# A fused attention and gated MLP kernel: v loaded as fp32 by SyncE and cast on chip, and every engine's order laid out anew

## The chip, the core and the metric

The kernel runs on one core of a Trainium2 chip. Its engines are TensorE (PE in the profile, with PEld for its weight loads), VectorE (DVE), ScalarE (ACT), GpSimd (POOL) and SyncE (SP, which here only issues transfers). The metric is the device time of one execution in microseconds (us), as the median of several runs.

## What is computed

The inputs are q, k and v of shape 8 x 12 x 448 x 64 (batch, heads, positions, width), two vectors of 64 weights, and the weights of a gated MLP. All are fp32.

```python
q_n, k_n = (rmsnorm(q, g_q), rmsnorm(k, g_k))          # x / sqrt(mean(x*x) + 1e-06) * g
scores = scale * np.matmul(q_n, k_n.transpose(0, 1, 3, 2))
attn = np.exp(scores - max); attn = attn / (sum + 1e-09)
x = np.matmul(attn, v)                                  # heads side by side: 8 x 448 x 768
h = np.maximum(x @ w_in, 0.0)
u, v = h[..., :512], h[..., 512:]
v_n = (v - mean) / np.sqrt(var + 1e-06)                 # over the 512
v_s = np.einsum('ts,bsd->btd', w_spatial, v_n) + b_spatial[None, :, None]
return ((u * v_s) @ w_out).astype(np.float32)
```

## The kernel before

The order of the work is written out by hand in one long string, PLAN (lines 20 to 152). Each word calls one function op_X, which issues the instructions of one step, and the tiles, their slots and PSUM banks stand in the word. An engine executes its instructions in the order of the words; between engines only data, reused slots and one helper, `port`, make anything wait. A word is `name.arguments/slots/engine`, with the engines a (ACT), v (DVE), g (POOL) and s (SP). So `N.13.1/0/g` normalizes input 1 (k) of group 13 into slot 0 on POOL.

Heads are worked on in 24 groups of 4 heads, three groups for each batch element. Group 0 is brought in by halves (small letters l, q, r, i, j, n, p, k). The steps of a group G:

- L (op_L, line 293): SP loads q (input 0) or k (input 1) of the group as fp32, 128 partitions x 896, into one of 9 slots `raw`. v comes by op_v (line 314): POOL requests it with a cast to bf16 on the way, straight into the tile `vt`, in one transfer for an even group and in two halves for an odd one.
- Q squares the tile (ACT, DVE or POOL), R sums over each 64 (DVE), I and J take a logarithm and an exponential on ACT, which give 1/rms. N (line 426) multiplies the tile by it and writes bf16 (`nrm`).
- T (line 481): SP issues a transposing transfer of `nrm` from SBUF to SBUF, into `qT` for q and into `kr` for k. Z (line 464 on DVE, 462 on ACT) multiplies `kr` by the weights of g_q and g_k and the scale into `kT`. Groups 0 to 3 are transposed by matmuls instead (P, p) and copied out by K, k.
- S (line 506): 8 matmuls of 64 x 32 give the scores of one unit, 128 x 896 in two PSUM banks. E (line 514): one ACT exponential of 128 x 896 writes bf16. There are 7 units in a group, so 168 of each.
- s, a and b (line 539): matmuls that sum the exponentials and multiply them by v, four to a pass. D and d (lines 558, 562) take 1/sum on ACT as exp(-ln), X (line 568) multiplies on DVE into `xt`.

The MLP of a batch element follows when its three groups are done: V and U (lines 584, 645) are matmuls with the two halves of w_in, c and u their ReLU evictions on ACT or DVE (575, 577), B and A the statistics and the normalization (620, 621, 636, DVE), M and m small ACT steps, H the matmuls with w_spatial (659), G the gating on DVE (664), O the matmuls with w_out (673), o their evictions (361, 363) and t the output transfers (690, SP). The last 64 of the 448 positions go through W (line 608), which works the V tail of one batch element beside the O tail of the one before it on two column halves of TensorE; the O tail lies in partitions 64 to 127.

z words (line 260) are dummy matmuls on an identity. setup (lines 245 to 254) fills constants and makes the identity on POOL. gA, gB, gC build the column of weights `g2_col` from two rows, which ACT's queue requests ahead of everything (241, 242). ws, wi, wo are POOL's casting loads of the weights, Y and y the transposes of w_spatial and their copies.

DVE and POOL steps that read and write SBUF call `port` (around line 284), which makes such a step wait for the last such step of the other engine in the order:

```python
def port(eng, inst):
    other = on_port.get("g" if eng is dve else "v")
    if other is not None:
        sync_dep(inst, other)
    on_port["v" if eng is dve else "g"] = inst
```

The steps that call it are Q, q, N, n on either engine, and A and Z on DVE.

Of the kernel before, what the change touches and what calls it, by code (L numbers as in the profile page):

```python
# [20 lines left out]
setup//v l.1.0/0 ws//g l.0.0/1 v.0.2//g L.1.0/2 v.0.1//g L.1.1/3 z.30/7 l.0.1 l.1.1 L.2.0/4 L.2.1/5 q.1.0/0/v L.4.1/6  # L21
gA//v gB/7 q.0.0/1/v L.3.1/7 z.33/6 r.0.0//v gC//v r.1.0//v Q.1.0/2/a L.4.0/8 i.0//a R.1.0//v j.0//a n.1.0//g
Q.1.1/2/a n.0.0//g p.1.0/7 z.7/6 q.0.1//a R.1.1//v q.1.1//g p.0.0/6 k.1.0/0/a Y.1/5 k.0.0/0/v I.1//a Y.3/7 J.1//a
r.1.1//v y.1//a Y.2/4 N.1.0/0/g Q.2.0/2/a r.0.1//v Y.0/5 y.3//v i.1//a y.2//v Q.2.1/0/a S.0.1/01 R.2.0//v N.1.1/1/g
S.0.0/23 L.3.0/2 j.1//a P.1.0/7 E.0.1/0/a R.2.1//v z.12/6 K.1.0/1/a n.1.1//g P.1.1/1 L.5.0/3 z.7/6 E.0.0/1/a K.1.1/1/v
n.0.1//g p.1.1/0 L.6.1/0 I.2//a S.1.6/67 k.1.1//v S.1.3/12 J.2//a S.1.1/34 L.5.1/1 E.1.6/2/a N.2.0/2/g z.3/f y.0//v
p.0.1/0 E.1.3/3/a S.1.0/67 k.0.1//v z.10/5 E.1.0/4/a v.0.0//g P.2.0/2 N.2.1/3/v L.6.0/4 z.4/5 E.1.1/5/a wi.1.1//g
s.1.0.0/7 S.1.2/01 Q.3.1/1/v wi.0.2//g P.2.1/6 E.1.2/6/a S.1.4/34 wi.1.0//g z.5/5 K.2.0/2/v E.1.4/7/a Q.4.0/2/g
S.0.3/01 K.2.1/2/v s.1.1.0 s.1.2.0 E.0.3/8/a s.1.3.0 R.3.1//v S.1.5/23 a.1.0.0/6 S.0.6/45 E.1.5/9/a a.1.1.0 Q.4.1/0/g
S.0.5/01 R.4.0//v a.1.2.0 E.0.6/a/a s.1.4.0 s.1.5.0 s.1.6.0 S.2.0/23 E.0.5/b/a b.1.0.0/5 wi.0.0//g Q.3.0/1/v b.1.1.0  # L30
b.1.2.0 b.1.3.0 v.0.3//g E.2.0/c/a S.2.2/01 a.0.0.0/4 a.1.3.0 R.3.0//v Q.5.0/2/g a.1.4.0 D.1/0/a a.1.5.0 a.0.1.0
E.2.2/d/a a.1.6.0 S.0.4/23 R.4.1//v z.4/7 I.3//a S.0.2/01 wi.0.1//g J.3//a E.0.4/e/a b.1.4.0 N.3.0/0/v b.1.5.0
wi.1.2//g b.1.6.0 s.0.0.0/7 E.0.2/f/a s.0.1.0 wi.0.3//g s.0.2.0 N.3.1/1/v S.2.4/23 s.0.3.0 wi.1.3//g z.2/b d.1//a
s.0.4.0 S.2.1/01 I.4//a s.0.5.0 X.1.1//v s.0.6.0 J.4//a z.5/b E.2.1/g/a N.4.1/2/g X.1.0//v P.3.0/5 D.0/1/a P.3.1/6
K.3.0/3/v E.2.4/h/a S.2.3/01 s.2.0.0/7 K.3.1/3/v s.2.1.0 N.4.0/3/g T.4.1/0 b.0.0.0/5 E.2.3/i/a b.0.1.0 R.5.0//v
b.0.2.0 s.2.2.0 b.0.3.0 d.0//a S.3.1/23 b.0.4.0 b.0.5.0 E.3.1/j/a Q.5.1/1/g S.2.5/01 T.4.0/1 b.2.0.0/6 b.2.1.0 b.0.6.0
E.2.5/k/a S.2.6/23 X.0.1//v a.0.2.0 z.2/b L.7.1/5 a.0.3.0 E.2.6/4/a b.2.2.0 Q.6.1/0/g R.5.1//v S.3.3/01 s.2.3.0
s.2.4.0 E.3.3/5/a s.2.5.0 S.3.0/23 a.2.0.0/5 a.2.1.0 I.5//a a.2.2.0 a.2.3.0 R.6.1//v J.5//a s.2.6.0 E.3.0/6/a
N.5.1/0/g a.0.4.0 a.2.4.0 a.0.5.0 a.0.6.0 Q.6.0/2/a b.2.3.0 a.2.5.0 X.0.0//v b.2.4.0 b.2.5.0 D.2/0/a b.2.6.0 R.6.0//v
N.5.0/1/g a.2.6.0 T.5.1/1 S.3.2/01 d.2//a S.3.4/23 U.0.2.0/7 E.3.2/3/a X.2.1//v U.0.2.1 V.0.1.0/4 X.2.0//v v.1.1//g  # L40
E.3.4/7/a T.5.0/0 V.0.1.1 Z.4/1/v V.0.1.2 I.6//a U.0.2.2 J.6//a c.0.1//v wb N.6.0/2/g S.4.5/01 S.4.0/56 L.7.0/2
u.0.2//v E.4.5/9/a W.0/4 L.8.1/7 E.4.0/2/a v.1.3//g T.6.0/2 S.4.4/23 c.0.3//v S.4.1/01 v.1.2//g S.4.2/56 E.4.4/1/a
U.0.0.0/7 B.0.1//v L.9.1/6 v.1.0//g U.0.0.1 E.4.1/8/a U.0.0.2 Z.5/0/v V.0.2.0/3 E.4.2/0/a N.6.1/3/g u.0.0//v V.0.2.1
S.5.1/01 S.3.5/45 wx//v S.5.6/67 E.5.1/e/a V.0.2.2 Q.7.1/1/g T.6.1/0 U.0.3.0/2 E.3.5/c/a c.0.2//v U.0.3.1 U.0.3.2
E.5.6/g/a L.8.0/8 S.5.5/01 u.0.3//v Q.7.0/0/g S.5.0/34 s.3.0.0/5 L.10.0/1 E.5.5/d/a s.3.1.0 B.0.3//v S.3.6/67 s.3.2.0
s.3.3.0 E.5.0/b/a s.3.4.0 R.7.1//v S.5.4/01 Q.8.1/2/g V.0.0.0/2 E.3.6/f/a V.0.0.1 R.7.0//v V.0.0.2 E.5.4/a/a s.3.5.0
s.3.6.0 c.0.0//v S.5.2/34 I.7//a b.3.0.0/7 b.3.1.0 J.7//a D.3/1/a b.3.2.0 B.0.0//v N.7.0/0/g a.3.0.0/2 s.4.0.1/10
d.3//a S.5.3/56 a.3.1.0 R.8.1//v s.4.1.1 E.5.3/i/a a.3.2.0 a.3.3.0 a.3.4.0 a.3.5.0 N.7.1/1/g B.0.2//v E.5.2/h/a
T.7.0/3 a.3.6.0 S.4.3/56 b.3.3.0 b.3.4.0 X.3.0//v b.3.5.0 M.0//a b.3.6.0 E.4.3/k/a S.4.6/34 X.3.1//v U.0.1.0/2
v.1.4//g T.7.1/1 m.0//a U.0.1.1 E.4.6/4/a Z.6/2/v wo//g s.4.2.1 s.4.3.1 A.0.2//v s.4.4.1 s.4.5.1 L.9.0/3 A.0.0//v  # L50
s.4.6.1 v.2.0//g A.0.3//v S.6.1/56 L.10.1/4 S.6.4/34 A.0.1//v U.0.1.2 v.2.2//g E.6.4/6/a H.0.0/7 v.3.1//g u.0.1//a
H.0.3/4 D.5/0/a G.0.0//v Q.8.0/1/g E.6.1/j/a H.0.1/2 G.0.3//v D.4/1/a S.6.0/56 G.0.1//v S.6.3/34 a.4.0.1/70 d.4//a
a.4.1.1 R.8.0//v a.4.2.1 E.6.0/3/a b.4.0.1/21 b.4.1.1 b.4.2.1 b.4.3.1 Z.7/3/v E.6.3/5/a b.4.4.1 b.4.5.1 b.4.6.1
Q.10.0/2/g a.4.3.1 d.5//a a.4.4.1 X.4.1//v S.7.3/56 S.7.0/34 I.8//a a.4.5.1 X.5.1//v E.7.3/7/a a.4.6.1 H.0.2/2
X.5.0//v Q.9.1/1/g Q.9.0/0/a X.4.0//v S.7.5/56 S.6.2/01 J.8//a G.0.2//v V.1.1.0/7 E.6.2/c/a R.10.0//v V.1.1.1
N.8.1/2/g V.1.2.0/2 E.7.5/f/a V.1.2.1 R.9.1//v E.7.0/2/a V.1.1.2 N.8.0/3/g V.1.2.2 T.8.1/0 R.9.0//v c.1.1//a S.7.4/01
# [97 lines left out]
"""  # L154


SLOTS = dict(raw=9, sqt=3, nrm=4, qT=4, kr=2, kT=4, et=21, rc=2, vs=2, vn=2, us=2, os=5)


@with_exitstack  # L160
# [572 lines left out]
```

## Time and profile before

| | |
|---|---|
| time, median of 3 runs | 285.55 us (282.64 to 287.17) |
| span of the profiled execution, first to last instruction | 277.8 us, 7.75 us under the median |
| first exponential starts | 18.56 us |
| last exponential starts | 232.5 us |
| granted TensorE clock, mean | 0.997 |
| transfers | 51.14 MB, mean 184 GB/s |

The profile is one execution. Its page gives the busy time of each engine and its share of the span, the span in 40 slices with the busy share in tenths, the groups of like instructions (busy time, mean duration of one in ns, then the idle time just ahead of them and what ended most of it), and the transfers by tile with the median time from issue to landing. The trace behind it answers further questions: who waited for whom, the chain of work that ended last, one tile's instructions, and stretches of time. Durations of overlapping instructions add up to more than the busy time of their engine. A busy TensorE is not at its peak, since matmuls are pipelined: 8 score matmuls that follow one another take 0.19 us, and 0.38 us alone.

### The profile page before, as it was taken

How to read it: one execution, taken by the hardware profiler on the slowest of the kernel's cores; microseconds unless marked ns; L12 is line 12 of the kernel's file. 1: busy time of each engine (PE TensorE's matmuls, PEld its weight loads, DVE VectorE, ACT ScalarE, POOL GpSimd, SP SyncE). 2: the span in 40 equal slices, each digit the busy share in tenths (PEclk: the TensorE clock that was granted, in tenths of full speed). 3: DMA queues.
4: the chain of work that ended last, by engine and by line, in shares of the span. 5: the costliest groups of instructions: out<-in, count | busy, mean ns of one | idle time of the engine just before them, and what ended most of it. 6: DMA issues, size and time to landing. Idle time of an engine off the chain costs nothing. (4 is left out here: it accounts for less than half of the span.)

```text
span 277.8 us, 10117 instructions
## 1 busy us (share of the span) xinstructions
PE 261.4 (94%) x4373; PEld 137.4 (49%) x4373; DVE 198.7 (72%) x351; ACT 216.8 (78%) x353; POOL 155.6 (56%) x130
## 2 busy tenths in 40 slices
PE   4799999979999999999999989999998999999993
PEld 4686464435545455354445444453553545455551
DVE  2478978695997997987995677966975174747740
ACT  1399999878999999998999979998898766420632
POOL 3287987987687598957875758645980000000000
PEclk9999999999999999999999999999999999999998
DMA  6989996999989999899999999966589400014586
GB/s 165 331 264 273 176 174 112 217 163 267 257 144 293 311 245 202 179 253 150 257 212 273 228 257 259 181 93 70 75 136 179 161 2 2 18 41 113 138 272 218
DMA packets 62967, 51.14 MB, mean 184 GB/s; under 512 B 39561, under 2 KB 58506, under 8 KB 62922
## 3 DMA queue, kind: packets, MB, share of 16 engines
q1 hardware_dynamic: 54690, 42.22, 64.5%
q0 software_dynamic: 8224, 8.27, 21.2%
q8 instruction: 34, 0.56, 0.8%
q14 instruction: 11, 0.09, 0.1%
q10 hardware_dynamic: 8, 0.00, 0.0%
HBM read 38.55 MB, written 11.01 MB: 178 GB/s over the span
## 5 line engine op out<-in xcount | busy, mean ns | idle before, releaser
L514 ACT ACTIVATE et<-ps 128x896 bf16<-128x896 f32 x168 | 145.7, 921 | 15.0 <-PE ps L506 13.4
L426 POOL TENSOR_TENSOR nrm<-raw,rs 128x896 bf16<-128x896 f32 x43 | 72.2, 1690 | 25.9 <-ACT rs L411 10.1
L506 PE MATMUL ps<-qT,kT 64*32 64x448 bf16 x1344 | 60.2, 354 | 2.5 <-DMA qT<-nrm 1.9
L382 POOL TENSOR_TENSOR sqt<-raw 128x896 f32<-128x896 f32 (+1 forms) x31 | 50.9, 1654 | 17.2 <-DVE vn L636 7.4
L393 DVE TENSOR_REDUCE ss<-sqt 128x14 f32<-128x896 f32 x46 | 48.4, 1075 | 5.0 <-ACT sqt L380 3.8
L539 PE MATMUL ps<-et,vt 64*32 64x448 bf16 x1344 | 48.4, 350 | 2.8 <-DMA vt<-in_v_dram 2.6
L645 PE MATMUL ps<-xt,w_in 128*128 128x448 bf16 x192 | 43.1, 353 | 0.0
L568 DVE TENSOR_TENSOR xt<-ps,rc 128x448 bf16<-128x448 f32 x48 | 28.3, 620 | 14.9 <-ACT rc L562 8.0
L673 PE MATMUL ps<-w_out,gt 128*128 128x384 bf16 x192 | 36.5, 326 | 0.1
L506 PEld LDWEIGHTS <-kT 64*32 64x32 bf16 x1344 | 21.5, 90 | 29.6 <-issue 22.0
L584 PE MATMUL ps<-w_in,xt 128*128 128x512 bf16 x144 | 35.6, 380 | 0.0
L539 PEld LDWEIGHTS <-vt 64*32 64x32 bf16 x1344 | 23.6, 92 | 17.3 <-DMA vt<-in_v_dram 3.9
L664 DVE TENSOR_TENSOR gt<-ps,us 128x448 bf16<-128x448 f32 x32 | 19.3, 620 | 13.0 <-PE ps L659 8.7
L361 ACT ACTIVATE os<-ps 128x384 f32<-128x384 f32 (+1 forms) x33 | 15.9, 493 | 15.4 <-PE ps L673 14.6
L659 PE MATMUL ps<-w_spT,vn 128*128 128x448 bf16 (+1 forms) x128 | 27.7, 353 | 0.0
L645 PEld LDWEIGHTS <-w_in 128*128 128x128 bf16 x192 | 17.0, 98 | 20.5 <-issue 7.3
L539 PE MATMUL ps<-et,ones 64*32 64x448 bf16 x672 | 26.2, 350 | 0.2 <-ACT et L514 0.2
L673 PEld LDWEIGHTS <-gt 128*128 128x128 bf16 x192 | 18.2, 98 | 15.4 <-issue 2.5
L314 POOL DMA_DIRECT2D vt<-in_v_dram x36 | 24.1, 673 | 0.0
L577 DVE TENSOR_SCALAR vs<-ps 128x512 bf16<-128x512 f32 (+1 forms) x24 | 16.3, 684 | 10.4 <-PE ps L584 6.8
L363 DVE COPY os<-ps 128x384 f32<-128x384 f32 (+1 forms) x31 | 16.9, 554 | 8.9 <-PE ps L673 7.7
L620 DVE BATCH_NORM_STATS2 s<-vs 128x6 f32<-128x512 bf16 (+1 forms) x32 | 21.9, 683 | 1.4 <-ACT vs L575 0.9
(62 smaller groups left out, 253.1 us busy)
## 6 DMA issues: line engine op xcount, KB each, us to landing
out_dram<-os SPq DMA_DIRECT2D x56, 192.0 KB, 3.2
raw<-in_q_dram SPq DMA_DIRECT2D x23, 448.0 KB, 5.5
raw<-in_k_dram SPq DMA_DIRECT2D x23, 448.0 KB, 7.0
vt<-in_v_dram POOLq DMA_DIRECT2D x24, 112.0 KB, 5.2
vt<-in_v_dram POOLq DMA_DIRECT2D x12, 224.0 KB, 7.0
w_in<-in_moe_w_in_dram POOLq DMA_DIRECT2D x8, 192.0 KB, 6.1
w_out<-in_moe_w_out_dram POOLq DMA_DIRECT2D x1, 768.0 KB, 11.3
raw<-in_k_dram SPq DMA_DIRECT2D x2, 224.0 KB, 2.6
```

Of the source, the lines that this page charges most:

```text
L314: pool.dma_start(out=vts[b % 2][64 * halves[0]:64 * halves[0] + 64 * len(halves), g].rearrange("p r c d -> p r (c d)"), in_=src)
L382: port(eng, eng.tensor_tensor(out=t, in0=x, in1=x, op=ALU.mult))
L393: dve.tensor_reduce(out=sss[G % 3][:, i].rearrange("p r c -> p (r c)"), in_=sqt[where.pop(("sq", G, i))].rearrange("p r (c d) -> p (r c) d ...
L426: port(eng, eng.tensor_tensor(out=nrm[sl[0]].rearrange("p c r d -> p r c d"), in0=raw[where["raw", G, i]].rearrange("p r (c d) -> p r c d" ...
L506: pe.matmul(out=ps[at:at + 32, sl[n], 0:S], lhsT=kT[64 * r:64 * r + 64, c, 64 * hh + 32 * x:64 * hh + 32 * x + 32], rhs=qT[64 * r:64 * r + ...
L514: act.activation(out=ets[sl[0]], in_=ps[:, a:b + 1:b - a, 0:S], func=AF.Exp, bias=0.0, scale=1.0)
L539: pe.matmul(out=ps[32 * l:32 * l + 32, where[kind, G][0], 0:S], lhsT=w, rhs=et_of(G, r, c)[at:at + 64], start=(n == 1), stop=(n == C), til ...
L568: dve.tensor_tensor(out=xts[b % 2][:, 2 * g + half, :], in0=ps[:, where.pop(("ab"[half], G))[0], 0:S], in1=rcs[where["rc", G]], op=ALU.mult)
L584: pe.matmul(out=ps[:, bank, :], lhsT=xts[b % 2][:, j, 128 * m:128 * m + 128], rhs=w_in[:, j % 2, j // 2, DH:], start=(n == 1 and j == 2 * ...
L645: pe.matmul(out=ps[:, bank, 0:S], lhsT=w_in[:, j % 2, j // 2, 128 * f:128 * f + 128], rhs=xts[b % 2][:, j, :], start=(n == 1 and j == 2 * ...
L659: pe.matmul(out=ps[:, sl[0], 0:S], lhsT=vns[b % SLOTS["vn"]][rows, m, 128 * f:128 * f + 128], rhs=w_spT[rows, m, :], start=(m == 0), stop= ...
L673: pe.matmul(out=ps[:, sl[0], 0:384], lhsT=gts[b % 2][:, f, 128 * m:128 * m + 128], rhs=w_out[:, f, 384 * h:384 * h + 384], start=(f == 0), ...
```

## The change

v is loaded as fp32 by SP into the slots of `raw`, as input 2 of op_L, and cast on chip into `vt` by a new step F. The two rows of g are requested by POOL behind the identity. w_sp no longer has a tile of its own but lies in the two tiles `gt` of the gating, and `raw` has 10 slots and `et` (the exponentials) 22. The O tail of the last batch element is worked in two column tiles, the first half of its columns in partitions 0 to 63 and the second in 64 to 127, and written out by two transfers. The list of words is new throughout. Counts of words that differ, by engine:

| step | before | after |
|---|---|---|
| L (loads of 448 KB) | 46 | 70, of which 24 are v (12 of them in two transfers) |
| v (POOL's casting loads) | 36 transfers | none |
| F (cast of v) | none | POOL 14, DVE 7, ACT 3 |
| N | POOL 43, DVE 3 | POOL 35, DVE 11 |
| n | POOL 4 | POOL 3, DVE 1 |
| Q | ACT 14, POOL 30, DVE 2 | ACT 9, POOL 32, DVE 5 |
| q | ACT 1, POOL 1, DVE 2 | ACT 3, DVE 1 |
| Z | ACT 2, DVE 18 | ACT 5, DVE 15 |
| K, y | ACT 1 each, DVE 5 and 3 | DVE 6 and 4 |
| c | ACT 8, DVE 24 | ACT 13, DVE 19 |
| u | ACT 9, DVE 23 | ACT 12, DVE 20 |
| o | ACT 33, DVE 31 | ACT 34, DVE 30 |
| dummy matmuls | 124 in 13 words, the last near exponential 20 | 63 in 2 words, at the start |

The new start of the list, and one stretch of the old and of the new list from the N of k of group 22 to its Z:

```
setup//v z.33/0 l.0.0/0 q.0.0/0/v r.0.0//v gl.1//g l.1.0/1 gl.0//g q.1.0/1/a gA//v r.1.0//v l.0.1 q.0.1//a r.0.1//v
i.0//a z.30/1 j.0//a gB/2 n.0.0//v p.0.0/3 L.1.0/2 Q.1.0/2/a L.1.1/3 R.1.0//v n.1.0//g Q.1.1/0/a k.0.0/0/a gC//v
p.1.0/4 R.1.1//v I.1//a J.1//a k.1.0/0/v S.0.1/56 S.0.2/07 ws//g N.1.1/0/v N.1.0/1/g S.0.0/13 P.1.1/2 Y.2/4 L.2.1/4
```

```
old: N.22.1/3/g s.18.0.1/75 s.18.1.1 E.21.2/a/a s.18.2.1 s.18.3.1 s.18.4.1 G.4.1//v s.18.5.1 s.18.6.1 S.21.1/01 c.5.1//v
v.6.1//g T.22.1/0 W.5/632 E.21.1/h/a B.5.1//v N.22.0/0/g D.18/1/a I.23//a O.3.2.1/1 D.19/0/a c.5.3//v J.23//a
...
S.21.5/67 u.5.0//v t.0.0 S.21.6/23 S.20.2/45 E.21.5/5/a Z.22/2/v

new: N.22.1/2/g a.18.5.1 a.18.0.1 S.21.4/06 S.21.3/12 b.18.4.1/75 a.18.4.1 I.23//a J.23//a N.23.0/3/g b.18.1.1 b.18.0.1
E.21.3/3/a X.18.0//v X.19.0//v b.18.3.1 b.18.6.1 b.18.2.1 E.21.4/e/a b.18.5.1 X.18.1//v S.21.6/12 E.21.6/f/a S.21.0/34
S.20.2/06 U.5.0.0/7 U.5.0.1 U.5.3.1/1 X.19.1//v E.20.2/2/a U.5.0.2 T.22.1/1 Z.22/1/v
```

The rest of the diff, cut to its core:

```diff
-SLOTS = dict(raw=9, sqt=3, nrm=4, qT=4, kr=2, kT=4, et=21, rc=2, vs=2, vn=2, us=2, os=5)
+SLOTS = dict(raw=10, sqt=3, nrm=4, qT=4, kr=2, kT=4, et=22, rc=2, vs=2, vn=2, us=2, os=5)
-    w_sp = const.tile([64, C, S], BF, name="w_sp")
+    w_sp = gt_all.rearrange("p n f s -> p (n f) s")[0:64, 0:C]
-        x = (q, k)[i]
+        x = (q, k, v)[i]
-    act.dma_start(out=g_row[:, 0], in_=bass.AP(tensor=g_q.tensor, offset=g_q.offset, ap=[[0, 1], [0, 2], [1, D]]))
-    act.dma_start(out=g_row[:, 1], in_=bass.AP(tensor=g_k.tensor, offset=g_k.offset, ap=[[0, 1], [0, 2], [1, D]]))
...
     def op_L(sl, e, G, i):
         b, g = divmod(G, NG)
         where["raw", G, i] = sl[0]
-        engines[e or "s"].dma_start(out=raw[sl[0]], in_=qk_rows(i, b, g))
+        rows = qk_rows(i, b, g)
+        if i < 2 or not flip(G):
+            engines[e or "s"].dma_start(out=raw[sl[0]], in_=rows)
+            return
+        for half in range(2):
+            src = bass.AP(tensor=rows.tensor, offset=rows.offset + (1 - half) * S * D,
+                          ap=[[C * D, 64], [2 * S * D, 2], [1, C * D]])
+            engines[e or "s"].dma_start(out=raw[sl[0]][64 * half:64 * half + 64], in_=src)
+
+    def op_gl(sl, e, i):
+        x = (g_q, g_k)[i]
+        engines[e].dma_start(out=g_row[:, i], in_=bass.AP(tensor=x.tensor, offset=x.offset, ap=[[0, 1], [0, 2], [1, D]]))
...
-    def op_v(sl, e, b, n):
-        g, halves = v_parts(b)[n]
...
-        pool.dma_start(out=vts[b % 2][64 * halves[0]:64 * halves[0] + 64 * len(halves), g].rearrange("p r c d -> p r (c d)"),
-                       in_=src)
+    def op_F(sl, e, G):
+        b, g = divmod(G, NG)
+        eng = engines[e]
+        dst = vts[b % 2][:, g].rearrange("p r c d -> p r (c d)")
+        src = raw[where["raw", G, 2]]
+        if eng is act:
+            copy(eng, dst, src)
+        else:
+            port(eng, eng.tensor_copy(out=dst, in_=src))
+        where["v", b, g] = {0, 1}
...
+    def tail_at(b, h):
+
+        return 0 if b == B - 1 and h == 0 else 64
...
                 h, f = divmod(n, 4)
-                todo.append(((n + 0.5) / 8, dict(
-                    out=ps[64:128, sl[h - 2], 0:384], lhsT=gts[(b - 1) % 2][:, f, TAIL:],
+                at = tail_at(b - 1, h)
+                todo.append(((f + 0.5 * h if b == B else n + 0.5) / 8, dict(
+                    out=ps[at:at + 64, sl[h - 2], 0:384], lhsT=gts[(b - 1) % 2][:, f, TAIL:],
...
-                    tile_position=(0, 64))))
+                    tile_position=(0, at))))
```

## The prediction

> **What bounds the kernel now.** I read the busy shares first, then the slices, then the waits, the windows, the tile views of the transposed q and k, and last the chain that ended last.
>
> ```profile
> span 277.8 us, 10117 instructions
> ...
> PE 261.4 (94%) x4373; PEld 137.4 (49%) x4373; DVE 198.7 (72%) x351; ACT 216.8 (78%) x353; POOL 155.6 (56%) x130
> ...
> ACT  1399999878999999998999979998898766420632
> POOL 3287987987687598957875758645980000000000
> ...
> DMA  6989996999989999899999999966589400014586
> ```
>
> TensorE shows 94%, but ScalarE (ACT) is at 9 tenths nearly everywhere from slice 2 to slice 33 and falls off only when the attention is over. So there are two stages: attention, in which ACT paces (168 exponentials of 0.92 us), and a last stage of matmuls alone. The DMA engines are nearly full for the first 170 us.
>
> ```profile
> L514 ACT ACTIVATE et<-ps 128x896 bf16<-128x896 f32 x168 | 145.7, 921 | 15.0 <-PE ps L506 13.4
> L426 POOL TENSOR_TENSOR nrm<-raw,rs 128x896 bf16<-128x896 f32 x43 | 72.2, 1690 | 25.9 <-ACT rs L411 10.1
> ...
> L382 POOL TENSOR_TENSOR sqt<-raw 128x896 f32<-128x896 f32 (+1 forms) x31 | 50.9, 1654 | 17.2 <-DVE vn L636 7.4
> ...
> L314 POOL DMA_DIRECT2D vt<-in_v_dram x36 | 24.1, 673 | 0.0
> ```
>
> The last number of a row is idle time ahead of it: ACT waited 13.4 us for scores. GpSimd (POOL) spends 24.1 us only on issuing the 36 loads of v.
>
> ```profile
> kr<-nrm SPq DMA_TRANSPOSE x20, 5.3
> qT<-nrm SPq DMA_TRANSPOSE x20, 4.8
> ```
>
> ```profile
> DMA to landing us min/median/max: 3.3/5.3/9.9
> ```
>
> The second fence is the tile view of kr, the transposed k: from issue to landing 3.3 us at best, 5.3 as a rule. This is the row on which the forecast rests.
>
> ```profile
> 202.32 3.35 POOL nrm L426 x2
> ...
> 207.85 7.97 DMA qT<-nrm
> ...
> 215.95 0.38 PE ps L506 x8
> ```
>
> That is the chain that ended last: POOL normalizes the last q, the transpose lands, scores start, and from there TensorE runs without a gap to the end. Behind the last exponential (232.5 us) there are only matmuls, evictions and 4 us of output transfer.
>
> **The change part by part.** The sum is made against the profiled execution: span 277.8 us. The median of the runs is 285.55, so 7.75 us lie around the span; I keep them.
>
> *Start, -5.5 us.* The first exponential starts at 18.56 now. Its scores were ready to start when the copy of q ended at 15.31, but 49 transposes of w_sp (3.42 us, from 14.58) stand ahead of them, and ACT could not take its first logarithm before it had squared a load that landed at 10.60. The new order sets both aside. It pays with the g rows: POOL requests them after the identity (1.63 us), and the VectorE (DVE) product that needs them stands ahead of the second sum r.1.0. Landed on the queue before they took until 8.18; from POOL I take the same to be safe (bounds: 4 us, the 2.6 us of the fastest small load after an issue at 1.7, and 8.2). Then 0.28 (product) + 0.61 (sum) + 0.29 + 0.21 (logarithm, exponential) + 0.93 (n on POOL) + 0.58 (transposes) + 0.68 (copy) + 0.38 (scores) give 12.2; the copy also stands behind the squares and sums of group 1, whose load is fifth and not third in line: 13. So 18.5 - 13 = -5.5, between -2.5 and -7.5. The 61 dummy matmuls that go (124 to 63, some 0.055 us each, 3.4 us) lay in gaps: nothing.
>
> *ACT, +6.5 us.* ACT loses 5 squares of 0.92 and one copy of 0.92 and one of 0.54; it gains 3 casts of v (F, at the 0.92 of the q copy), 3 Z at 1.04, 5 c at 0.59, 3 u at 0.54, one o at 0.49, two half squares of 0.56 and the bias row (0.54). That is -6.1 + 12.6 = +6.5. By the order ACT has 1.5 less ahead of the first exponential and 0.9 more behind the last, so +7.1 lies between. Durations overlap (their sum over the kernel is 235, busy 216.8), so x0.92: +6.5. ACT is 91% busy there, so it is paid in full.
>
> *DVE and POOL.* DVE: 8 N more at 1.09, 3 squares at 1.08, 7 casts (no row; between 0.45 of a bf16 row and 1.09 of N; midway, 0.77), less 5 c, 3 u, 3 Z and small ones: about +10, 198.7 to 209. POOL: -24.1 (issues), -13.5 (8 N), -1.8 (a half square and a half N), +1.7 (a square), +1.2 (two issues), and 14 casts (between 0.94 of a half-size row and 1.69; N has the same input and output tile, so 1.69): +23.7, in all 142.8. Neither is full. But the helper `port` lets no port operation of one of them start before the last one of the other in the order: N, squares and n on either, A and Z on DVE, now F too. By rows this chain holds 153.5 us now (126.8 POOL, 26.7 DVE) and 182 afterwards.
>
> *v on SyncE.* 24 loads become 36 issues on SP of some 0.5 us: 18 us beside about 118 that it has, no bound. Packets: 0.115 us on the software queue (21.2% of 16 engines, 8224 packets), 0.081 for plain loads in the first 20 us; 6144 of them cost the engines between 13 us less and nothing. Covered by ACT.
>
> *The new orders: +10 us.* The order is one list; the exponentials in it are a clock of 0.87 us. I counted ACT work between the word that normalizes k (N) and the word Z that scales the landed transpose, for groups 4 to 23. Now it is 7.2 to 21.4 us, median 10.8. In the new list it is 2.4 to 11.7, median 5.3; group 19 falls from 11.1 (10 exponentials) to 4.4 (3), 20 from 14.0 to 3.8, 22 from 10.7 to 3.7, 23 from 10.9 to 2.4. Between lie N itself (1.69 on POOL, 1.09 on DVE) and issue to landing. At 5.3 us that needs 7.0 or 6.4: no group is short now, 15 are then, by 30.7 us together. At 3.3 us seven are short, by 8.0. Loads tighten too: between a load of q or k and its square lie 11 exponentials now, 4 then (3.5 us, against a median landing of 6.1). A late transpose holds DVE at Z; behind it wait x, c, u and the sums R on DVE, by `port` the next N, square or cast on POOL, and then the scores and ACT. Part of it is caught up, since POOL has idle time and runs ahead of the list: I take half of the middle, (30.7 + 8.0) / 4 = 9.7, say 10; bounds 0 and 30.7.
>
> *End, -1.6 us.* Matmul work behind the last exponential falls from 39.4 to 38.0 us by the list (fewer U, more O), -1.4. The last W runs its 8 tail matmuls in two column tiles side by side: 1.43 us becomes about 0.7, but its two evictions on ACT (0.49 each) now come one after the other, and the tail goes out in two transfers: -0.2.
>
> Sum: 277.8 - 5.5 + 6.5 + 10 - 1.6 = 287.2, or +9.4; on the median 295.0 us.
>
> **The rivals.**
>
> *B, the transposes land in time.* POOL and SP don't follow the list's clock; where they run ahead, or the landing stays at its 3.3 us, at most half of 8.0 is paid: 277.2 to 281.2, so 285.0 to 289.0. For it: nothing in the waits of before shows DVE held by kr for more than 0.2 us. Against: the median landing, with DMA at 9 tenths. [...]
>
> *C, faster.* From exponential 133 (185.1 us) to the last (232.5) pass 47.4 us, with 37.4 of ACT work by rows; the 10 us between go to POOL's late N of the last groups (the chain above). POOL has 12.8 us less to do and no issue of v between these N any more (four of 0.65 now, from 195.69); if they come early, the loss goes: 277.2 - 10 = 267.2, so 275.0. It decides if the N of groups 21 to 23 end 7 us ahead of their Z. Against: in the new list the last N of k stands 2.4 us ahead.
>
> *D, nothing is caught up.* The chain of port operations is 182 of some 205 us, so POOL can't run ahead, and every shortfall is paid: 277.2 + 30.7 = 307.9, so 315.7. Against: POOL's own work, 142.8 us, leaves it idle a third of the stage.
>
> **How the numbers follow.** The forecast 0.42 (its own range 289 to 304), B 0.25, C 0.16, D 0.17. Differences under 2% (279.8 to 291.3) can hardly be told from no change here. Faster by over 2%: C, 0.16. Within: B and the lower edge of the forecast, 0.27. Slower: the rest, 0.57. With a tenth left out on each side the range goes from 277 to 312.
>
> **What would show it.** First exponential near 13 us (the start). ACT busy near 223. Waits "DVE kT on DMA kr" and "PE ps on DMA qT" that sum to over 10 us where they are 0.2 and 1.9 now: the stalls. L314 gone, POOL near 143. Where those waits stay under 3 us and the last exponential starts before 228, the forecast is wrong by its largest term, and B or C holds; where the first exponential is no earlier than 16, the g rows took the gain.

## The result and the profile after

The changed kernel takes 388.21 us (median of 4 runs, 386.71 to 391.32) beside 286.02 us for the kernel before: 1.367 times as long (95% interval 1.352 to 1.382). The forecast of 295.0 had the direction, but only a tenth of the size, and its range ended at 312. Executions of one kernel differ by a few us, often with the mean clock that TensorE is granted (0.97 to 1.00 for most of the kernel before), so the ratios here and below are taken over the faster executions of each kernel and the medians over all of them, and the clock is given where a comparison hangs on it.

The page of the changed kernel, the lines that answer to those shown of before:

```profile
span 386.4 us, 10053 instructions
...
PE 285.2 (74%) x4312; PEld 140.4 (36%) x4312; DVE 208.4 (54%) x358; ACT 229.5 (59%) x364; POOL 134.6 (35%) x102
...
PE   6477986777567676667867767766776767699994
...
ACT  4465688247657553757765675757668567542353
POOL 3355655422716413445552443353137220000000
...
DMA  7948619680684438417592873955657913000587
```

The engines did nearly the same work: ACT 229.5 us after 216.8, DVE 208.4 after 198.7, POOL 134.6 after 155.6. But the span grew by 108.6 us. ACT stood at 9 tenths through the attention; now ACT and TensorE stand mostly at 5 to 7 tenths side by side, from slice 5 to slice 34, and no other engine is full instead, nor are the DMA engines for more than single slices. No engine became the bound. Each is waiting.

For whom, the waits say (engine, line and tile that waited, then who released it; us in total, times, longest us). Lines moved with the change: E, the exponentials, is now L521, the scores S L513, the passes s, a and b L546, X L575, V L591, H L671.

```profile
ACT et L521 <- PE ps L513: 44.0, 45, 3.7
...
ACT et L521 <- PE ps L546: 28.0, 20, 4.9
...
DVE xt L575 <- PE ps L546: 26.9, 15, 6.2
PE ps L546 <- ACT et L521: 25.3, 29, 1.8
...
PE ps L513 <- ACT et L521: 19.5, 21, 1.7
DVE vs L584 <- ACT et L521: 17.4, 4, 12.0
```

The second line is the strange one. An exponential reads scores; what L546 writes are the sums and the products with v, in other banks, which no exponential reads. Yet ACT waited 28.0 us for L546. Before the change, its waits for L539 (as that line was then) came to 0.8 us between 30 and 233 us. And TensorE waited 19.5 us to write scores until an exponential was done, where the kernel before has 2.5 us of idle time ahead of its scores in all, most of it for a transposed q.

The chain of work that ended last shows what this looks like in order of time (start, length, what):

```profile
152.60 0.50 PE ps L513 x16
153.10 1.20 PE ps L546 x46
154.30 0.02 issue
154.32 1.73 ACT et L521 x2
156.05 0.04 issue
156.09 1.50 PE ps L546 x52
157.60 0.23 PE ps L513 x4
157.83 0.02 issue
157.85 0.93 ACT et L521
158.78 0.04 issue
158.82 0.99 PE ps L546 x32
```

TensorE and ACT take turns. Scores and passes run to 154.30, then two exponentials alone, then passes, then one exponential alone, then passes. Work of the two engines that lay side by side before lies end to end now. The summary of the chain has it for the whole kernel:

```profile
PE 57%; ACT 30%; issue 5%; DMA 3%; DVE 3%; ACTq 0%; POOL 0%; SPq 0%; DVEq 0%; POOLq 0%
```

The cause stands in the words, and neither the table of the change nor the prediction had looked there. E reads the two banks of a unit in one instruction, `ps[:, a:b + 1:b - a, 0:S]`: bank a, then bank b, with a step of b - a. In the old list, the two banks of all 168 units are neighbours. In the new list 27 are; 56 lie 2 apart, 35 lie 3 apart, and 50 lie 4 to 7 apart. The theory: what orders the instructions takes such a read for all that lies from a to b. Then E waits for the last matmul that wrote a bank in between, and the next matmul into one of those banks waits for E. The semaphore waits that are written into the two programs when they are built, ahead of any run, bear this out: in the old program exponentials wait for TensorE 145 times, 143 of them for scores and 2 for dummies; in the new one 135 times, 95 for scores and 40 for other matmuls (24 for passes, 7 for V, 5 for U, 2 for H, one each for O and the transposes of w_sp).

### The profile page after: what moved, and what is told of

Its sections match the earlier page's. It is cut to its first block, busy times and chain, and to the rows that moved or that the text cites. A ratio compares the mean times of both kernels' runs of the same rounds, so it can differ in the third digit from the quotient of the medians.

```text
span 386.4 us, 10053 instructions
## 1 busy us (share of the span) xinstructions
PE 285.2 (74%) x4312; PEld 140.4 (36%) x4312; DVE 208.4 (54%) x358; ACT 229.5 (59%) x364; POOL 134.6 (35%) x102
## 4 chain that ended last, share of the span: by engine, by line
PE 57%; ACT 30%; issue 5%; DMA 3%; DVE 3%; ACTq 0%; POOL 0%; SPq 0%; DVEq 0%; POOLq 0%
ACT et L521 27%; PE ps L546 13%; PE ps L513 9%; PE ps L657 8%; PE ps L685 8%; PE ps L591 7%; PE ps L671 6%; PE ps L620 3%; DMA gt<-in_moe_w_spatial_dram 2%; DVE xt L575 2%; PE ps L355 1%; PE ps L452 1%; DMA raw<-in_k_dram 1%; ACT vs L582 0%; PE ps L460 0%
## 5 line engine op out<-in xcount | busy, mean ns | idle before, releaser
L521 ACT ACTIVATE et<-ps 128x896 bf16<-128x896 f32 x168 | 148.9, 916 | 103.2 <-PE ps L513 44.0
L433 POOL TENSOR_TENSOR nrm<-raw,rs 128x896 bf16<-128x896 f32 x35 | 58.8, 1689 | 98.5 <-ACT rs L418 27.7
L513 PE MATMUL ps<-qT,kT 64*32 64x448 bf16 x1344 | 64.6, 382 | 22.5 <-ACT et L521 19.5
L389 POOL TENSOR_TENSOR sqt<-raw 128x896 f32<-128x896 f32 x32 | 53.5, 1680 | 41.6 <-DVE kT L471 13.9
L546 PE MATMUL ps<-et,vt 64*32 64x448 bf16 x1344 | 51.0, 368 | 13.5 <-ACT et L521 13.1
L657 PE MATMUL ps<-xt,w_in 128*128 128x448 bf16 x192 | 45.5, 359 | 6.5 <-ACT et L521 6.5
L575 DVE TENSOR_TENSOR xt<-ps,rc 128x448 bf16<-128x448 f32 x48 | 28.4, 620 | 36.5 <-PE ps L546 26.9
L591 PE MATMUL ps<-w_in,xt 128*128 128x512 bf16 x144 | 41.1, 403 | 8.8 <-ACT et L521 8.7
L513 PEld LDWEIGHTS <-kT 64*32 64x32 bf16 x1344 | 20.8, 92 | 53.3 <-issue 47.0
L546 PE MATMUL ps<-et,ones 64*32 64x448 bf16 x672 | 29.6, 378 | 12.1 <-ACT et L521 12.1
L671 PE MATMUL ps<-w_spT,vn 128*128 128x448 bf16 (+1 forms) x128 | 29.2, 363 | 9.9 <-ACT et L521 9.9
L546 PEld LDWEIGHTS <-vt 64*32 64x32 bf16 x1344 | 23.9, 95 | 32.0 <-issue 23.3
L584 DVE TENSOR_SCALAR vs<-ps 128x512 bf16<-128x512 f32 (+1 forms) x19 | 13.0, 686 | 34.3 <-ACT et L521 17.4
L368 ACT ACTIVATE os<-ps 128x384 f32<-128x384 f32 (+1 forms) x34 | 16.2, 491 | 23.7 <-PE ps L685 13.7
L657 PEld LDWEIGHTS <-w_in 128*128 128x128 bf16 x192 | 17.7, 98 | 28.9 <-issue 14.9
L685 PEld LDWEIGHTS <-gt 128*128 128x128 bf16 x192 | 18.7, 99 | 22.2 <-issue 9.6
L591 PEld LDWEIGHTS <-xt 128*128 128x128 bf16 x144 | 14.1, 103 | 28.4 <-issue 18.2
```

Of the source, the lines that this page charges most:

```text
L389: port(eng, eng.tensor_tensor(out=t, in0=x, in1=x, op=ALU.mult))
L433: port(eng, eng.tensor_tensor(out=nrm[sl[0]].rearrange("p c r d -> p r c d"), in0=raw[where["raw", G, i]].rearrange("p r (c d) -> p r c d" ...
L513: pe.matmul(out=ps[at:at + 32, sl[n], 0:S], lhsT=kT[64 * r:64 * r + 64, c, 64 * hh + 32 * x:64 * hh + 32 * x + 32], rhs=qT[64 * r:64 * r + ...
L521: act.activation(out=ets[sl[0]], in_=ps[:, a:b + 1:b - a, 0:S], func=AF.Exp, bias=0.0, scale=1.0)
L546: pe.matmul(out=ps[32 * l:32 * l + 32, where[kind, G][0], 0:S], lhsT=w, rhs=et_of(G, r, c)[at:at + 64], start=(n == 1), stop=(n == C), til ...
L575: dve.tensor_tensor(out=xts[b % 2][:, 2 * g + half, :], in0=ps[:, where.pop(("ab"[half], G))[0], 0:S], in1=rcs[where["rc", G]], op=ALU.mult)
```

## Experiments

**Neighbouring banks in the new order.** Only the digits of banks are dealt anew, by a search over the lifetimes of the banks, so that every pair of a unit is next to each other; words, order, engines and slots stay.

```diff
-p.1.0/4 R.1.1//v I.1//a J.1//a k.1.0/0/v S.0.1/56 S.0.2/07 ws//g N.1.1/0/v N.1.0/1/g S.0.0/13 P.1.1/2 Y.2/4 ...
+p.1.0/7 R.1.1//v I.1//a J.1//a k.1.0/0/v S.0.1/56 S.0.2/34 ws//g N.1.1/0/v N.1.0/1/g S.0.0/12 P.1.1/0 Y.2/7 ...
```

> The changed kernel, its list of words in the same order word for word; only the PSUM bank digits are dealt anew, so that the two banks of a score unit are always neighbours. In the changed kernel they are neighbours in 27 of 168 units, in the kernel before in all 168. Theory: an exponential that reads two banks with others between them is made to wait for whatever was last written to the banks between, and whoever writes there next waits for it, so that ScalarE and TensorE take turns. Then the waits of exponentials on matmuls other than scores (L546, L591, L657: 28.0 + 5.8 us and more) and those of other matmuls on exponentials (25.3 + 9.9 + 8.7 + 8.2 + 6.5 us) go, and the time falls from 388 us to between 280 and 310 us. Rival one, the short leads of transposes and loads that the prediction rested on: banks have no part in that, the time stays within 2% of 388. Rival two, the order itself lets TensorE's queue put other work ahead of the scores: again the time stays above 370.

Measured: 291.36 us (288.40 to 295.75), 1.0215 of before (1.0057 to 1.0374). From its page and its groups (busy us and mean ns of one, then the idle time before them and who ended it):

```profile
span 288.7 us, 10027 instructions
...
PE 256.7 (89%) x4295; PEld 135.1 (47%) x4312; DVE 207.0 (72%) x358; ACT 223.4 (77%) x364; POOL 134.6 (47%) x102
...
L521 ACT ACTIVATE et<-ps 128x896 bf16<-128x896 f32 x168 | 146.3, 922 | 22.4 <-PE ps L513 21.4
...
L322 POOL CAST vt<-raw 128x896 bf16<-128x896 f32 x14 | 12.8, 930 | 15.5 <-DMA raw<-in_v_dram 3.5
```

97.7 us of span are gone with nothing but the bank numbers, and ahead of the exponentials stands a wait for scores. In its program 136 exponentials wait for TensorE, 135 of them for scores. What the rest of the change costs is the difference between this kernel and the one before.

**Spread banks in the old order.** The other direction: banks 0 to 7 renamed to 0, 2, 4, 6, 1, 3, 5, 7. All uses of a bank move together, so that reuse is as it was; only the distance in a pair changes, to 2 for 152 units and 5 for 16.

```diff
-        a, b = where.pop(("S", G, u))
+        a, b = sorted(where["S", G, u])
+        swap = int(where.pop(("S", G, u))[0] > a)
...
+        where["swap", G, u] = swap
```

> The kernel before, its list of words in the same order; only the eight PSUM banks are renamed one for one (0 to 7 become 0, 2, 4, 6, 1, 3, 5, 7), so that every true dependence stays and no score unit has neighbouring banks (distance 2, in some 5). Where a unit's first bank comes second in number, the two halves of its exponential change places. Theory of the bank pairs: the same turn-taking appears in the old order, the time rises from 286 us to 350 us or more, and waits of exponentials on matmuls other than scores appear, which are near zero now (0.8 us). Both rivals: nothing but names changes, so 286 us within 1%.

Measured: 339.33 us (336.94 to 340.63), 1.193 of before (1.183 to 1.204). The groups of this kernel (E is L516, the passes are L542):

```profile
L516 ACT ACTIVATE et<-ps 128x896 bf16<-128x896 f32 x168 | 148.6, 916 | 61.2 <-PE ps L506 27.2 <-PE ps L542 11.2 <-PE ps L648 4.8
L542 PE MATMUL ps<-et,vt 64*32 64x448 bf16 x1344 | 50.9, 350 | 13.6 <-ACT et L516 13.1 <-DVE xt L571 0.4
```

The same pattern, put into the kernel before: exponentials wait 11.2 us for passes and 4.8 for U, and passes 13.1 us for exponentials. In its program 140 exponentials wait for TensorE, 49 of them for matmuls other than scores. It costs 55 us against 97 in the new list, less than I had expected. That would fit a dose (here there is one bank in between in nine units of ten, there up to six), which no run varies by itself. The granted clock is not what costs the 55 us: it was 0.975 to 0.986 in these runs, and 0.967 to 0.999 with the same banks and the reads cut (below). In the changed kernel it was 0.909 to 0.922, and 0.950 to 0.976 with neighbouring banks, so a part of the 97 us may come by way of the clock; how much was not measured.

**The exponential cut in two.** Two runs ask whether it is the reach of the one read or the banks themselves. Each exponential becomes two over one bank each; every bank stays where it is.

```diff
-        act.activation(out=ets[sl[0]], in_=ps[:, a:b + 1:b - a, 0:S], func=AF.Exp, bias=0.0, scale=1.0)
+        for n, bank in enumerate((a, b)):
+            act.activation(out=ets[sl[0]][:, n], in_=ps[:, bank, 0:S], func=AF.Exp, bias=0.0, scale=1.0)
```

In the new list, with its own spread banks:

> The changed kernel with its own banks, each exponential of 128x896 over two banks cut into two of 128x448 over one bank each. Theory of the bank pairs: nothing reads across banks any more, so the turn-taking goes; ScalarE pays for 168 more instructions, each half some 0.55 us by the rows of 128x448 (0.548 and 0.579) for 0.92 whole, so 168 x 0.18 = 30 us more work on ScalarE; 310 to 335 us. Rivals: the waits stay and ScalarE has more to do, so 388 us or more, up to 415.

And in the old list with the spread banks of the run above:

> The kernel before with the banks renamed as in the run of that kind (339.33 us), and each exponential over a bank pair cut into two over one bank each. Same banks, same matmuls, same order; only the access that reaches over the banks between is gone, at 168 more ScalarE instructions (busy time of the exponentials 157 us in place of 149 in the changed kernel when cut so). Theory (what lies between the two banks of a pair is waited for): back to 285 to 300 us. Rival (the banks' reuse, not the reach of the access, makes the waits): stays above 325.

Measured: 291.36 us for the first (one run), 288.90 us for the second (285.25 to 290.32; 1.018 of before, 1.007 to 1.030). The group of the exponentials, in the first

```profile
L522 ACT ACTIVATE et<-ps 128x448 bf16<-128x448 f32 x336 | 156.9, 575 | 18.0 <-PE ps L513 17.2
```

and in the second:

```profile
L517 ACT ACTIVATE et<-ps 128x448 bf16<-128x448 f32 x336 | 156.4, 577 | 14.3 <-PE ps L506 11.9 <-PE ps L543 1.6
```

With the reach gone the loss is gone (96.9 and 50.4 us), on the same banks and with 168 more instructions. Of the 272 exponentials that wait for TensorE in the first program, 270 wait for scores. That settles the cause: the waits come from the span of one strided access, not from which bank is reused when; data, reused slots and `port` are not all that makes an engine wait. Cutting costs little: 8.0 us more of busy time than in the changed kernel (156.9 against 148.9). I had expected 310 to 335 and paid every one of those instructions at the end; most of it lay beside other work. In the engine's own time one read of 0.916 us stands for two of 0.575. In the kernel's time joined reads were faster only in the old list and with neighbours (283.9 us, against 288.9 cut and on spread banks); in the new list joined reads of neighbours are no faster than cut ones (291.4 both), and joined reads of spread banks take 388.2.

**What is left of the change: the start.** From here on the parent is the new list with neighbouring banks. Its first exponential starts at 13.2 us (18.6 before), but the thirteenth at 31.9 (30.6 before): what was gained is lost within twelve exponentials. The stretches of the parent (window, its length, busy us and instructions of each engine, then the granted clock):

```profile
0.00:10.00 10.00, 6.25 (x72) 5.83 (x72) 5.01 (x15) 4.41 (x7) 2.67 (x9) 1.00 0.79 256
10.00:15.00 5.00, 3.38 (x36) 1.65 (x37) 4.23 (x6) 3.74 (x7) 2.33 (x3) 0.69 1.10 380
15.00:20.00 5.00, 1.70 (x20) 1.37 (x18) 1.21 (x2) 3.14 (x6) 4.34 (x5) 0.50 1.03 228
20.00:25.00 5.00, 5.00 (x61) 3.75 (x61) 2.59 (x5) 2.31 (x4) 0.88 (x1) 0.50 0.79 248
```

Two suspects: TensorE stands still from 15.5 to 18.8, waiting for w_spatial, which landed at 18.7; and its clock is down to half from 11.9 to 25.6 us, after it had been idle by turns since 7 us. One run each.

```diff
-... gB/2 n.0.0//v p.0.0/0 ... p.1.0/7 ... P.1.1/0 Y.2/7
+... gB/2 z.24/4 n.0.0//v p.0.0/0 z.8/4 ... p.1.0/7 z.22/4 ... P.1.1/0 z.60/7 Y.2/7
```

> The changed kernel with neighbouring banks (291.36 us, span 288.7), with 114 more dummy matmuls put into the four idle stretches that TensorE shows between 7.9 and 18.8 us: 24 behind the g column, 8 behind the first transposes of group 0's q, 22 behind those of k, and 60 ahead of the first transposes of w_spatial. In its parent the granted clock falls from 1.00 to 0.50 at 11.9 us and comes back at 25.7; before the change it stays at 1.00 there. Theory (the low clock alone costs what the early start gained): the clock stays at 1.00, the 24 matmuls of the first scores take 0.76 us and not 2.43, the sixteenth exponential comes some 3 to 5 us earlier, and the span ends at 284 to 286. Rival one (the late w_spatial, landing at 18.7, sets this stretch, whatever the clock): under 1.5 us, span 287 to 289. Rival two (the dummies only get in the way): span 289 to 291.

```diff
-... gl.0//g q.1.0/1/a ... S.0.2/34 ws//g N.1.1/0/v
+... gl.0//g ws//g q.1.0/1/a ... S.0.2/34 N.1.1/0/v
```

> The same parent with one word moved: w_spatial is requested from GpSimd right behind the two g rows and not behind the first scores, so its request stands at about 3 us and not at 10.2. No dummy is added. Theory (low clock): w_spatial lands some 8 us earlier and TensorE's idle stretch of 3.3 us from 15.5 goes, but TensorE is still idle by turns between 7 and 12 us, so the clock still falls; 2 to 4 us less, span 285 to 287. Rival one (the wait for w_spatial is the whole loss): 5 us less, span near 284. Rival two: 0.8 MB more among the first loads delay q and k of group 0 by up to 2 us, the first exponential comes at 14 to 15 us in place of 13.2, and the span is 288 to 290.

Measured: 292.38 us with the dummies (1.024 of before, 1.013 to 1.034) and 290.14 with w_spatial early (1.024; 1.015 to 1.034): neither can be told from the parent's 1.0215. With w_spatial early the first exponential comes at 15.4 and not at 13.2, as rival two had it: beside the large load the small ones land later (VectorE's product of the rows of g starts at 8.2 us and not at 7.1). TensorE no longer stands still for w_spatial, yet the thirteenth exponential starts at 31.7 (31.9 in the parent): that wait is not the whole loss. With the dummies, the clock stays at 1.00 past 12 us as intended, and in the profiled execution it falls at 21.2 us:

```profile
20.00:21.00 1.00, 1.00 (x18) 0.90 (x14) 0.68 (x2) 0.00 (x0) 0.37 (x1) 1.00 1.06 253
21.00:22.00 1.00, 1.00 (x23) 0.67 (x29) 1.00 (x2) 0.00 (x0) 0.00 (x0) 0.62 1.08 360
22.00:24.00 2.00, 2.00 (x28) 1.27 (x13) 0.90 (x3) 1.94 (x4) 0.00 (x0) 0.50 0.73 272
24.00:26.00 2.00, 2.00 (x28) 1.13 (x26) 1.35 (x4) 1.10 (x3) 1.01 (x1) 0.50 0.09 33
```

In this execution the experiment moved the low stretch and didn't remove it. In two others it can hardly have been there: a granted mean of 0.996 leaves room for some 2 us at half the clock (an estimate, 0.004 of 286 us, at half the rate). Their spans are 285.6 and 287.3 us, still above the kernel before at 0.994 to 0.997 (277.0 to 282.7). So the low clock is not all of what is left. What it costs stays open: the four runs at 0.962 to 0.975 took 288.8 to 296.3 us, but the parent has a run of 286.4 us at 0.954.

**The lead of the transposes, by itself.** The largest term of the prediction, put into the kernel before: the words N of k move towards Z, with their transposes where these would stand ahead of them, and nothing else. Nineteen groups are moved so; of group 20:

```diff
-c.4.2//a S.16.3/67 N.20.1/3/g S.18.4/01 E.16.3/c/a
+c.4.2//a S.16.3/67 S.18.4/01 E.16.3/c/a
...
-S.16.5/01 E.17.4/d/a T.20.1/0 U.4.3.0/2 R.21.1//v
+S.16.5/01 E.17.4/d/a U.4.3.0/2 R.21.1//v
...
-u.4.1//v U.4.0.1 I.21//a U.4.0.2
+u.4.1//v U.4.0.1 N.20.1/3/g T.20.1/0 I.21//a U.4.0.2
```

> The kernel before, its banks and everything else kept, with the words that normalize k (19 of the groups 4 to 23) moved towards the scaling of the landed transpose, until the ScalarE work between them is what the changed order has, as far as the reuse of buffers allows: median 5.8 us in place of 10.8 (5.3 in the changed order); 13 groups fall short of 7.0 us, by 26.3 us together. The prediction's largest term by itself: +10 us (0 to 30.7), so about 295 beside 285 for the kernel before, with VectorE's waits for the transposed k growing by some 10 us. Rival (GpSimd runs ahead of the list, so that the transposes are issued early in time whatever their place): within 2 us of the kernel before, those waits under 4 us.

> The run with short leads in the old order (306.74 us; it normalized the k of one group, 15, with the factors of group 18) with that one word put back before the word that overwrites the factors: median lead 6.1 us, 13 groups short of 7.0 us, by 25.3 together. The prediction's term: some 295 to 305, with VectorE's waits for the transposed k near 20 us. Rival (the one misplaced word made the loss of that run): within 4 us of the kernel before.

Measured: 306.74 us (1.086; 1.077 to 1.095) with one word misplaced, so that group 15's k was normalized with the wrong factors, and 305.09 us (302.96 to 310.49; 1.080, 1.067 to 1.093) with that word put back. Of the waits of the second:

```profile
DVE kT L464 <- DMA kr<-nrm: 18.3, 7, 5.1
```

Together with ACT's, 20.1 us are spent waiting for the transposed k, where the kernel before has 0.2, and the run is 21 us longer. So the mechanism exists, at about 0.8 us per us of shortfall (21 of 25.3), and it was undervalued if anything. Now the other way, in the parent, with the slots of `nrm` dealt anew where the moves ask for it (group 22; its transpose then stands 48 words ahead of Z):

```diff
-d.19//a J.22//a H.4.3/2
+d.19//a J.22//a N.22.1/3/g H.4.3/2
...
-o.4.3.1//v N.22.1/2/g a.18.5.1
+o.4.3.1//v a.18.5.1
...
-U.5.0.2 T.22.1/1 Z.22/1/v
+U.5.0.2 Z.22/1/v
```

> The changed kernel with neighbouring banks (291.36 us), with the normalization of k of groups 4 to 23 put right behind the word that gives its factors, and its transpose some 2 us of ScalarE work later: median lead 10.0 us of ScalarE work in place of 5.3 (10.8 before the change). From issue to the scaling of the landed transpose its parent shows 4.9 us (median) against 8.9 before. The prediction's term, as it was sized: 10 us less, 281. As VectorE and ScalarE's waits of 4.8 us for the transposed k in the parent have it: up to 5 us less, 286 to 291. Rival (normalizations that come earlier hold up squares on GpSimd and loads on SyncE's queue): slower, 292 to 298.

Measured: 330.07 us (327.34 to 332.55), 1.167 of before (1.158 to 1.175). The waits for the transposed k did fall, to 1.0 us, and from issue to scaling passed 10.5 us in place of 4.9. What came in their place:

```profile
ACT et L521 <- PE ps L513: 45.8, 34, 7.6
...
POOL vt L322 <- DMA raw<-in_v_dram: 15.2, 5, 7.8
...
POOL sqt L389 <- DMA raw<-in_q_dram: 12.9, 2, 11.4
POOL sqt L389 <- DMA raw<-in_k_dram: 12.7, 6, 4.3
```

The rival holds, and more strongly than I had put it. On SyncE's queue a transpose that stands early waits there for its normalization (84.3 us for normalizations on POOL in all, 50.7 in the parent), and the loads behind it wait with it: POOL waits 40.8 us for raw q, k and v (18.1 in the parent). Lengthening the leads alone, in this way, cost more than the waits it took away.

**ACT's share, and the v part alone.**

```diff
-c.0.0//a Z.7/3/a u.1.1//a ... F.19//a F.21//a F.22//a
+c.0.0//v Z.7/3/v u.1.1//v ... F.19//g F.21//g F.22//g
```

> The same parent with 14 words given to another engine: three casts of v go from ScalarE to GpSimd; three scalings of k, five relus c and three relus u from ScalarE to VectorE. Order, banks and loads stay. ScalarE loses some 9.7 us (223.4 to 214), VectorE gains 6.6 (207 to 213.6), GpSimd 2.8. If ScalarE paces this kernel, as the prediction's term of 6.5 us has it: 6 to 9 us less, 282 to 285. Rival (TensorE, VectorE and the waits between them pace it, and ScalarE is one of several at nine tenths): within 2 us of 291. Rival two (VectorE becomes the bound): 293 to 297.

```diff
+        dst = vts[b % 2][:, g].rearrange("p r c d -> p r (c d)")
+        if not flip(G):
+            pool.dma_start(out=dst, in_=rows)
+            return
...
-            port(eng, eng.tensor_copy(out=dst, in_=src))
```

> The same parent with the v part alone undone: at the place of each load of v GpSimd requests it with the cast in the transfer, straight into the tile that the matmuls read, and the 24 casts on chip are left out (one load is put behind the last reader of its buffer). GpSimd loses 12.8 us of casts and gains 24.1 of issues, VectorE loses 4.4, ScalarE 2.9; SyncE issues 36 fewer transfers. By the prediction (v on SyncE costs nothing, casts are paid on ScalarE alone): about 2.7 us less, 288 to 290. Rival (GpSimd, freed of the issues, is what lets the normalizations run ahead of short leads in the changed kernel): the waits for the transposed k grow from 4.8 us to over 10, and the time is 295 to 302.

Measured: 299.67 us with ACT's work taken off (1.061; 1.054 to 1.067), 300.77 us with v requested by POOL (1.066; 1.059 to 1.072). Both are some 8 to 9 us slower than the parent. The first lies outside all three ranges that were expected. In it, ACT's busy time fell to 216.6 us, and waits grew:

```profile
ACT et L521 <- PE ps L513: 33.5, 39, 4.5
...
POOL vt L322 <- PE ps L513: 21.0, 4, 13.9
...
POOL vt L322 <- DMA raw<-in_v_dram: 9.7, 3, 8.2
DVE kT L471 <- DMA kr<-nrm: 9.1, 8, 3.6
```

The second line names the wrong releaser. The program lets these casts wait for no scores, and the passes that they do wait for stand some 1500 to 2100 instructions earlier. The longest, 13.9 us, is the cast for group 22, POOL's last instruction: it starts at 248.09, right behind VectorE's normalization A (to 247.96), which `port` puts ahead of it, and nothing on POOL stands behind it. What holds others up is in the third line: the cast for group 21, now on POOL, waits 8.2 us there for its load, the normalization of group 23's k stands behind it (231.67), and VectorE then waits 3.6 us for that transposed k. In the second run:

```profile
PEld L543 <- DMA vt<-in_v_dram: 10.9, 3, 5.1
DVE kT L468 <- DMA kr<-nrm: 10.8, 7, 4.2
```

Here TensorE waits for v itself and the waits for the transposed k double, as the rival said, though the places of the loads had been laid out for SyncE. Taking 6.8 us off ACT's busy time did not shorten this list. But the moved casts brought waits of their own, so the run doesn't price ACT's work by itself, and whether ACT's busy time sets the end of this list stays open. In both runs, what an instruction holds up in its queue weighed more than the work that was moved.

**The two ends in the old order.** The last run tries the parts that had looked like gains in the kernel before.

```diff
-... l.0.0/1 v.0.2//g L.1.0/2 v.0.1//g L.1.1/3 ... n.0.0//g p.1.0/7
+... l.0.0/1 L.1.0/2 L.1.1/3 ... n.0.0//g v.0.2//g v.0.1//g p.1.0/7
...
-                    tile_position=(0, 64))))
+                    tile_position=(0, at))))
```

> The kernel before, its order and banks kept, with the two parts of the change that the runs so far show as gains tried alone: at the start the two loads of v (112 KB in bf16 each, read as fp32) that stand among the first q and k are requested behind the first normalization of q, so that ScalarE's wait of 6.7 us for a load of q that landed at 10.6 is shorter; at the end the last tail runs in two 64-column tiles, as in the changed kernel. Theory (what the change gains is at its two ends, what it loses lies between): the first exponential 1 to 2 us earlier, the end behind the last exponential 0.5 to 1 us shorter, in all 1.5 to 3 us less: 281 to 283 beside 284. Rival (ScalarE's next words are not earlier, since other loads set them): within 1 us.

Measured: 282.50 us beside 284.19, a ratio of 0.994 (0.990 to 0.998; 12 runs against 17). It is the fastest of all kernels here, by 0.6%. Its profile doesn't say why: the first exponential starts at 18.6 as before, the wait for q is 6.3 us and not 6.7, and the last W is shorter but the span behind the last exponential is not (46.0 us, 45.3 before). I call the gain measured, small as it is, and its cause open.

## Why the prediction was wrong, step by step

**The step that failed** is the sum's list of terms. It followed the order of the words and their engines, and costed the new orders at their transposes alone ("The new orders: +10 us"). The same words also carry PSUM banks, and those were taken as given. With the banks as they are, the profiled span is 108.6 us above before; with neighbouring banks 10.9, so 97.7 us belong to a term that the sum didn't have: exponentials that wait for matmuls in the banks between, and matmuls that wait for exponentials. No rival had it either. That the forecast had the direction is luck as far as these 97.7 us go, since none of its terms made them. Rival D came nearest in time (315.7), by another mechanism. The sign that the prediction named for its own theory, waits for the transposed k of over 10 us, is absent from the changed kernel: 0.6 us. "Where those waits stay under 3 us ... the forecast is wrong by its largest term" was right about the first half; but the last exponential came at 342.7 us and not before 228, a case that the text had no place for.

**The rest of the sum**, read from the kernel with neighbouring banks: span 288.7, forecast 287.2. That is a near hit of which only some terms are confirmed, and it is partly luck: the start's gain wasn't kept, and the +10 came at half.

One step under the whole sum was wrong too. The prediction took the 7.75 us between the profiled span and the median for time around the span. In all the runs here the time is only 1.7 to 2.6 us above the span of the same execution; the rest is that the profiled execution of before, at 277.8, was one of its shortest (277.0 to 291.7 in 46 others, median 282.4). So the 10.9 us of span overstate what the change costs with neighbouring banks. The medians of the runs give 7.0 us (291.36 against 284.32; the ratio's interval 1.6 to 10.6), where +9.4 was forecast.

- *Start, -5.5.* The first exponential: 13.20 (forecast 13; 12.18 in the changed kernel). The term is right as a time of that instruction. It wasn't kept: by the thirteenth exponential all 5.4 us of it are lost and 1.3 more, while w_sp is late (18.7 us) and the clock is down (0.50).
- *The dummies: nothing.* Not confirmed. Before, the clock was 1.00 throughout this stretch. Adding 114 brought no time back that could be measured, though in two of six runs the low stretch can hardly have been there.
- *ACT, +6.5.* Busy 223.4 against 216.8: +6.6. That it is paid in full is not confirmed: taking 6.8 us off again made the kernel 8.3 us slower, by waits of the moved casts among others.
- *DVE and POOL.* DVE 207.0 (forecast 209). POOL 134.6 (142.8): POOL's cast of v takes 0.930 us, the lower bound (0.94) and not the 1.69 of N, which has the same tiles but a second input. 14 of them: 13.0 us, not 23.7. DVE's cast takes 0.63 (0.77 taken), ACT's 0.95 (0.92).
- *v on SyncE: nothing.* Better than that in this list: putting v back on POOL, at the places laid out for SyncE, costs 9.4 us (300.77 against 291.36).
- *The new orders, +10.* From issue to scaling the transposes of k have 4.9 us (median) against 8.9 before, so the halving was read rightly from the lists. Landing takes 4.0 us (median) and not 5.3, and the waits come to 4.8 us in place of 0.2. The mechanism was right and the waits were half the size. In the changed kernel, where the packets fill 57.6% of the span of the 16 DMA engines (86.6% before), the tile view of kr has

```profile
DMA to landing us min/median/max: 2.9/3.0/4.7
```

Even there no transpose of k landed in less than 2.9 us (3.3 before).

- *End, -1.6.* 45.3 us behind the start of the last exponential became 43.5 with neighbouring banks and 43.7 in the changed kernel. Right. The last W takes 0.84 us after 1.49.

Of the 10.9 us between the two profiled spans, the rows account for the lost start (6.6 up to the thirteenth exponential, less the 5.4 gained), some 4.6 more of waits for the transposed k and 6.3 more of ACT's work between first and last exponential (200.0 against 193.7 us), less 1.8 at the end. These overlap. Which of them would give time back was not settled, since each attempt to change one alone made another wait.

## What to carry to other kernels

When a change deals buffers anew, list the addresses that each instruction spans, from first to last byte, and not only those that it touches: here reads with a stride over two banks waited for matmuls in the banks between (28.0 us for passes), neighbouring banks took 97.7 us off the span, and the semaphore waits of the built program, which stand there ahead of any run, show it (40 of 135 for matmuls other than scores). In the profile the sign was an engine that waited for an instruction whose result it doesn't read, and two engines at about six tenths that took turns on the chain that ended last (PE 57%, ACT 30%). In these lists, fitted by hand, a term that was right by itself (a lead, an engine's load) brought its gain only as far as what was queued behind the moved words allowed (330.07 and 299.67 us against 291.36).

## What the runs showed of the hardware

Two exponentials of 128 x 448 take 0.575 us each (new list, cut) where one of 128 x 896 takes 0.916 (changed kernel); with waits around them, 168 more instructions cost the kernel 5 us (288.9 on spread banks against 283.9 in the old list) or nothing that could be measured (291.4 against 291.4 in the new).

TensorE's granted clock was 0.50 from 11.6 to 32.1 us in the run with w_spatial early, with TensorE busy without a gap from 14.4 on. In the run with more dummies it fell to 0.50 at 21.2 us, with TensorE busy from 18.5, and came back at 34.9; in their parent it came back at 25.6, with TensorE busy from 18.8. So TensorE had been busy for 17.7, 16.4 and 6.8 us when the clock came back; what brings it down and back was not shown.

In the new list with neighbouring banks, on POOL a cast with one input takes 0.930 us where a product with a second input, from and into tiles of the same size, takes 1.688.
